# A chunked RWKV-7 recurrence feeding a cosine-gated unit, on one core: sign products in four column pieces, two loads in another order, three slots moved from one chunk to the next

## The chip, the cores and the metric

The kernel runs on one core of one Trainium2 chip. Its time is the device time of one execution in microseconds (us). Seven executions of the kernel before gave a median of 821.45 us (818.95 to 823.89). One further execution was taken with the hardware profiler; all views of the profile come from that one.

## The reference, cut to what matters

Two blocks in a row. The first is a recurrence over 768 time steps for 4 batches and 8 heads with a 40 x 40 state each; the second takes its output as 3072 tokens of 320 values.

```python
for t in range(S):                                    # r, k, v, w, a, b: (4, 8, 768, 40), float32
    y[:, :, t] = np.einsum('bhd,bhde->bhe', rt, state)
    Sa = np.einsum('bhde,bhe->bhd', state, at)
    state_decay = state * wt[:, :, None, :] - np.einsum('bhd,bhe->bhde', Sa, bt)
    state = state_decay + np.einsum('bhd,bhe->bhde', vt, kt)
...
x = np.ascontiguousarray(attn_out.transpose(0, 2, 1, 3)).reshape(B * S, H * D)
h = x @ w_in                                          # w_in: (320, 2048), float64
g = h * np.cos(h)
return (g @ w_out).astype(np.float32)                 # w_out: (2048, 320), float64
```

## The kernel before, in words

**Chunks.** The 768 steps are cut into 24 chunks of 32. Within a chunk the recurrence is written as small matrix products (heads and batches packed into the PE array) and one triangular inverse. `main(c)` (line 821) lists the five steps of a chunk: `ch_t` transposes the state `qz`, `ch_q` multiplies it with r, `ch_x` makes the right-hand side `x0`, `ch_s` (line 601) multiplies it with the inverse `rt`, `ch_z` (line 627) makes the new state and the output. In `ch_z`, DVE adds the PSUM result to `qz` (line 654), then POOL multiplies it by the chunk's decay (line 655), and the next chunk's `ch_t` needs that product.

**Preparation.** `p1(c)` (line 784) prepares two chunks at once from w, a and b: `p1_w` (line 358) transposes w (for chunks under 4 it also scans it on DVE), `p1_a` transposes a and takes the reciprocal of w (line 389) with the product b times reciprocal on POOL (line 390), `p1_b` transposes that product, `p1_n` multiplies both. `p2(c)` does the like for v, r and k. From chunk 4 on, w comes as a running product that `ws_scan` makes for four chunks at a time and stores to DRAM.

**The inverse.** `inverse(c)` (line 480) inverts the triangular matrices of four chunks together on DVE: one transpose, 31 steps of two DVE instructions (lines 466 and 470), one transpose back into `rt`. That of chunks 4 to 7 can start when `p1_n(6)` is done, and `ch_s(4)` needs its end.

**The second block** works on the 256 tokens of two chunks (a group g) and on a quarter j of the 2048 columns. It is cut into pieces, which run in one fixed order: `first_a(g, j)` and `first_b(g, j)` (8 and 16 matrix instructions into `ph`, then the cosine on ACT and DVE), and, once the next pair is under way, `second(g, j, 0)` and `second(g, j, 1)` (8 into `po` each). Below they are A(g,j), B(g,j), S(g,j)0 and S(g,j)1. A group may start only two chunks after its first chunk (`allowed`, line 914).

**The weights** come as float64. `rounded` (line 220) turns them into float32 in 20 work units of 128 x 512 values: a load of both 32-bit words, mantissa and exponent on DVE (lines 241, 242, 251) and ACT (lines 245, 254), the sign on ACT (line 247, a bf16 tile), the product of mantissa and exponent on DVE (line 257), and the product with the sign, in place, on POOL (line 260).

**The order of the work** is written by hand, and every engine runs its own instructions in that order. For each chunk a list `segs` (lines 924 to 960) names the steps; `M` is a slot for one piece of the second block. `step` (line 342) runs a step, then whatever was put off with `later(n, ...)`, then as many steps of the inverse and of the weights as `fill` says: (2, 3) in chunk 3, (2, 0) in chunk 4. Before `ch_s`, while `rt` is not there yet, the loop at line 972 takes further pieces, with four steps of the inverse each. Chunks above 3 have a goal for the pieces done by their end; by the end of chunk 5 it is 30.

**Loads.** `load(c, n)` (line 146) issues four DMAs of 40 KB, one per batch, by default on SP's queue. At the kernel's start SP issues w(0), w(1), then the six loads of line 186, then k, v and r of chunk 0; ACT issues a(0), a(1) and one load of w as a whole (`ws_fetch(1)`); POOL issues a(2) and a(3). A load into a buffer waits until its last reader is done: w(6) and w(7) follow the reciprocals of w(4) and w(5), and SP issues w(7), a(6), b(6), a(7), b(7) in this order.

Of the kernel before, what the change touches and what calls it, by code (L numbers as in the profile page):

```python
# [12 lines left out]
ALU = mybir.AluOpType  # L13
# [7 lines left out]
def kernel(  # L21
# [43 lines left out]
    nc = tc.nc  # L65
    B, H, S, D = r.shape
    P, C, DP = 128, 32, 64
# [52 lines left out]
    for n, fill in (("w", 1.0), ("a", 0.0), ("b", 0.0)):  # L120
        for i in range(4):
            x = slice((i - 2) * H * DP, (i - 1) * H * DP)
            if i < 2:
                t = const.tile([P, H, DP], F32, tag=f"nat_{n}{i}", name=f"nat_{n}{i}")
            else:
                t = {
                    "w": w_in_sb[:, 0, late:], "a": w_in_sb[:, 1, late:], "b": late_out
                }[n][:, x].rearrange("p (h d) -> p h d", h=H)
# [4 lines left out]
    for n in "kvr":  # L133
        t = const.tile([P, H, D], F32, tag=f"nat_{n}", name=f"nat_{n}")
# [11 lines left out]
    def load(c, names, via=nc.sync):  # L146
        for n in names:
            for i in range(B):
                at_c = src[n][i, :, c * C : (c + 1) * C, :]
                if n == "w" and c >= 4:  # L150
                    at_c = wd[c // 4][i, :, c % 4]
                via.dma_start(nat[n, c][blk[i], :, :D], at_c.rearrange("h t d -> t h d"))  # L152
# [6 lines left out]
    def ws_fetch(q, via=nc.sync):  # L159
        n = 4 * C * D  # L160
        via.dma_start(
            ws.rearrange("p t d -> p (t d)"),
            bass.AP(w.tensor, w.offset + q * n, [[S * D, B * H], [C * D, 4], [1, C * D]]),
        )

    def ws_scan(q):
        n = 1
        while n < C:
            to = ws[:, 2 * n - 1 :: 2 * n]
            nc.vector.tensor_tensor(to, to, ws[:, n - 1 :: 2 * n], ALU.mult)  # L170
            n *= 2
        n = C // 4
        while n:
            to = ws[:, 3 * n - 1 :: 2 * n]
            nc.vector.tensor_tensor(to, to, ws[:, 2 * n - 1 : C - 1 : 2 * n], ALU.mult)
            n //= 2
# [6 lines left out]
        load(c, "w")  # L183
        load(c, "a", nc.scalar)
    ws_fetch(1, nc.scalar)
    for n, c in (("b", 0), ("b", 1), ("w", 2), ("w", 3), ("b", 2), ("b", 3)):
        load(c, n)
    load(0, "kvr")

# [27 lines left out]
    WID = 512  # L217
    first_done, second_done = [], []

    def rounded(m, dst, src, by, by_sb):  # L220

        pool, tag = (
            ((sb2, "gT"), (sb2, "gT"), (sb1, "nt"), (sb1, "u"), (sb1, "inv"))[m % 5]
            if m < 10 else ((sb1, "nt"), (sb1, "u"), (sb1, "inv"))[(m - 10) % 3]
        )
        t = {}

        def fetch():  # L230
            t["words"] = pool.tile([P, WID, 2], I32, tag=tag, name="words")
            for rows, cols, part in src:
                nc.sync.dma_start(
                    t["words"][rows, cols].rearrange("p n w -> p (n w)"), part.bitcast(I32)
                )

        def taken():
            hi = t["words"][:, :, 1]
            t["mant"] = sb2.tile([P, WID], I32, tag="mant", name="mant")
            t["expo"] = sb2.tile([P, WID], I32, tag="expo", name="expo")  # L240
            nc.vector.tensor_scalar(t["mant"], hi, 0xFFFFF, None, ALU.bitwise_and)
            nc.vector.tensor_scalar(
                t["expo"], hi, 20, 0x7FF, ALU.logical_shift_right, ALU.bitwise_and
            )
            nc.scalar.activation(t["expo"], t["expo"], ACTF.Relu, bias=to_bits, scale=2.0**23)
            t["sign"] = sb2.tile([P, WID], mybir.dt.bfloat16, tag="sign", name="sign")
            nc.scalar.activation(t["sign"], hi, ACTF.Sign)

        def mantissa():
            frac = t["mant"].bitcast(F32)  # L250
            nc.vector.scalar_tensor_tensor(
                frac, t["words"][:, :, 0].bitcast(U32), 2.0**-32, t["mant"], ALU.mult, ALU.add
            )
            nc.scalar.activation(frac, frac, ACTF.Identity, bias=by_sb, scale=2.0**-20 * by)

        def product():
            nc.vector.tensor_tensor(
                dst, t["mant"].bitcast(F32), t["expo"].bitcast(F32), ALU.mult
            )
            nc.gpsimd.tensor_tensor(dst, dst, t["sign"], ALU.mult)  # L260

        return fetch, taken, mantissa, product

# [75 lines left out]
    def later(steps, work):  # L339
        waiting.append([steps, work])  # L340
# [465 lines left out]
    def scanned(q):  # L806

        ws_scan(q)
        later(2, lambda: ws_store(q))
        if q + 1 < NCH // 4:  # L810
            later(12, lambda: ws_fetch(q + 1))
# [17 lines left out]
    with tc.manual_schedule():  # L829
# [53 lines left out]
        v, k, g = p2(0)  # L883
# [33 lines left out]
        M = object()  # L917
        for c in range(NCH):
            t, q, x, s, z = main(c)
            v, k, g = p2(c + 1) if c + 1 < NCH else [lambda: None] * 3  # L920
            q0 = c - c % 4 + 4
            fill, pn, pn4 = (1, 4), None, None
            if c == 0:
                segs = [s, z]
            elif c == 1:
                segs = [t, v, q, k, x, g, s, z]
            elif c == 2:
                segs, fill = [t, v, q, k, M, x, M, g, M, s, M, z, M, M], (0, 2)
            elif c == 3:
                pw4, pa4, pb4, pn4 = p1(4)  # L930
                pw, pa, pb, pn = p1(6)
                segs = [
                    t, pw4, M, q, pa4, M, x, lambda: scanned(2), M, s, pw, M, pb4, pa, M, pn4, M, z, M,
                    pb, v, pn, k, M, g,
                ]
                fill = (2, 3)
            elif c == 4:
                pw, pa, *p8 = p1(8)
                segs = [t, v, M, q, M, k, x, M, g, M, M, M, s, pw, z, M, pa, lambda: scanned(3), M]
                fill = (2, 0)  # L940
            elif c == 5:
                pw, pa = p1(10)[:2]
                pb, pn = p8
                segs = [t, M, pb, q, M, pn, k, M, x, M, s, pw, v, M, z, M, g, M, pa, M]
            elif c % 4 == 0 and q0 < NCH:
                pb, pn = p1(q0)[2:]
                segs = [t, v, M, q, M, k, x, M, g, M, s, pb, M, z, M, pn, M, M]
                if q0 + 4 < NCH:
                    segs.insert(-1, lambda: scanned(c // 4 + 2))
            elif c % 4 == 1 and q0 < NCH:  # L950
                pw, pa = p1(q0 + 2)[:2]
                segs = [t, M, pw, q, M, x, k, M, s, v, M, z, M, pa, M, g, M, M]
            elif c % 4 == 2 and q0 < NCH:
                pb, pn = p1(q0 + 2)[2:]
                segs = [t, M, pb, q, M, pn, v, M, x, M, s, k, M, g, M, z, M, M]
            elif c % 4 == 3 and q0 + 4 < NCH:
                pw, pa = p1(q0 + 4)[:2]
                segs = [t, M, pw, q, M, x, k, M, s, v, M, z, M, pa, M, g, M, M]
            else:
                segs = [t, v, M, q, M, x, k, M, g, M, s, M, M, z, M, M]  # L960
            n = len(segs)

            goal = 8 * (c + 1) - (18 if c < 19 else 20)
            empty, places = 0, segs.count(M)
            if c > 3:
                empty = max(0, min(places - (goal - done), 2 if c < 8 else places))
                goal = max(goal, done + places - empty)
            place = 0
            if c == 19:
                shifted(N_PAD[c])  # L970
            for i, seg in enumerate(segs):
                while seg is s and ("rt", c) not in G:
                    if allowed(c):
                        piece(4, 0)
                    else:
                        inv_steps.pop(0)()
                while seg is pn4 and w_steps:
                    w_steps.pop(0)()
                if seg is not M:
                    step(seg, *fill, small=seg in (q, x, g, s, z, pn, pn4))  # L980
                    if c < 2 or c == 2 and not done:
                        busy({s: 6, q: 5, v: 4, k: 4, z: 4}.get(seg, 3))
                else:
                    place += 1
                    if place * empty // places > (place - 1) * empty // places:
                        continue
                    if allowed(c) and (c != 4 or done < 23):
                        piece(*fill)
                while i == n - 1 and c > 3 and done < goal and c != 4 and allowed(c):
                    piece(*fill)  # L990
                if seg is pn and (c == 3 or c > 4 and c % 4 == 2):
                    inv_steps.extend(inverse(q0))
# [36 lines left out]
```

## Time and profile before

| | |
|---|---|
| median of seven executions | 821.45 us |
| the profiled execution, its own time | 820.94 us |
| its span, first to last instruction | 819.2 us |
| mean granted TensorE clock | 0.953 |
| PE busy | 741.1 us, 90% |
| DVE busy | 509.6 us, 62% |
| ACT busy | 383.9 us, 47% |
| POOL busy | 201.0 us, 25% |
| the 20 sign products on POOL | 1.15 to 1.61 us each |

Of the PE's idle time, 68.5 us lie in the first 260 us and 9.6 us in the remaining 559. A row of a timeline has the start and the duration in us, the engine, the line, the operation, what it writes and reads, shapes and count; in brackets stand the idle time of the engine before it and what released it. Durations include the time in which an instruction is held up at its operands. "SPq" rows are the issuing of DMAs.

### The profile page before, as it was taken

What the parts mean: (1) busy time and instruction counts of PE and PEld (TensorE: products, weight loads), DVE (VectorE), ACT (ScalarE), POOL (GpSimd) and SP (SyncE); (2) the same over time, 40 slices, a digit from 0 to 9 for tenths busy, and PEclk for the clock granted to TensorE, in tenths of its full rate; (3) what the DMA queues carried; (4) which work ended last, traced back from release to release, by engine and by line L of the source; (5) the groups of instructions that cost most, each with busy time, mean ns of one, the idle gap of its engine ahead of it and who ended that gap; (6) DMA issues with size and microseconds to landing.
All of it is one profiled execution on the core that took longest, in us unless ns stands there. A gap on an engine that the chain in (4) does not pass through costs nothing.

```text
span 819.2 us, 37665 instructions
## 1 busy us (share of the span) xinstructions
PE 741.1 (90%) x16832; PEld 567.3 (69%) x16832; DVE 509.6 (62%) x1081; ACT 383.9 (47%) x707; POOL 201.0 (25%) x352
## 2 busy tenths in 40 slices
PE   3647778799688999999999999999999999999997
PEld 2533456677566777787777877877787777777775
DVE  6988888869644698454797553895445873332231
ACT  1214776554254545446345545435635435363352
POOL 5215554430203123221230330330230222201000
PEclk9757799999699999999999999999999999999999
DMA  7466553254043323334223324223220212101000
GB/s 120 69 147 175 162 150 118 47 126 69 25 101 87 68 45 63 63 95 77 50 39 69 67 62 69 60 43 68 53 42 23 45 37 53 22 17 37 20 17 16
DMA packets 183297, 55.66 MB, mean 68 GB/s; under 512 B 157152, under 2 KB 178656, under 8 KB 183136
## 3 DMA queue, kind: packets, MB, share of 16 engines
q1 hardware_dynamic: 180560, 51.95, 29.2%
q8 instruction: 132, 2.16, 1.1%
q10 hardware_dynamic: 2320, 0.98, 0.6%
q0 software_dynamic: 256, 0.33, 0.2%
q14 instruction: 29, 0.24, 0.1%
HBM read 42.07 MB, written 11.14 MB: 65 GB/s over the span
## 4 chain that ended last, share of the span: by engine, by line
PE 60%; DVE 20%; DMA 6%; ACT 5%; issue 3%; SPq 3%; POOL 2%; DVEq 0%; ACTq 0%; POOLq 0%
PE ph L101 21%; PE po L101 19%; DVE inv_tmp L466 4%; DVE inv L470 4%; PE dps L101 3%; PE x0ps L101 3%; SPq L152 3%; DVE rw L389 3%; PE gram L101 2%; PE vT L326 2%; PE sps L101 2%; DVE turns L730 1%; PE qps L101 1%; DMA xT<-xd 1%; PE nps L101 1%
## 5 line engine op out<-in xcount | busy, mean ns | idle before, releaser
L101 PE MATMUL po<-w_out_sb,gT 128*128 128x320 f32 x768 | 224.2, 440 | 0.0
L101 PE MATMUL ph<-xT,w_in_sb 128*128 128x256 f32 x768 | 186.5, 388 | 4.5 <-DVE gT L738 3.8
L101 PEld LDWEIGHTS po<-w_out_sb,gT 128*128 128x128 f32 x768 | 140.8, 191 | 55.0 <-issue 2.8
L101 PEld LDWEIGHTS ph<-xT,w_in_sb 128*128 128x128 f32 x768 | 140.8, 192 | 32.9 <-issue 13.8
L728 ACT ACTIVATE turns<-ph,rnd 128x512 f32<-128x512 f32 x96 | 63.9, 686 | 152.8 <-PE ph L101 152.4
L730 DVE SCALAR_TENSOR_TENSOR turns<-turns,ph 128x512 f32<-128x512 f32 x96 | 63.8, 684 | 107.5 <-ACT turns L728 107.1
L738 DVE TENSOR_TENSOR gT<-ph,turns 128x512 f32<-128x512 f32 x96 | 65.7, 686 | 36.1 <-ACT turns L735 36.1
L655 POOL TENSOR_TENSOR qz<-qz,wc 128x160 f32<-128x160 f32 x92 | 43.0, 485 | 161.0 <-DVE qz L654 160.2
L470 DVE TENSOR_TENSOR inv<-inv,inv_tmp 128x31 f32<-128x31 f32 (+15 forms) x186 | 72.6, 390 | 6.4
L466 DVE TENSOR_TENSOR inv_tmp<-u,inv 128x31 f32<-128x31 f32 (+15 forms) x186 | 70.4, 378 | 4.4
L734 ACT ACTIVATE turns<-turns 128x512 f32<-128x512 f32 x96 | 60.1, 626 | 24.6 <-DVE turns L730 24.6
L735 ACT ACTIVATE turns<-turns,half_pi 128x512 f32<-128x512 f32 x96 | 69.3, 722 | 3.1
L488 POOL COPY vp<-nat_v 128x320 f32<-128x320 f32 x25 | 12.1, 483 | 199.1 <-DMA nat_v<-in_v_dram 182.6
L101 PE MATMUL ph<-xT,w_in_tail 64*128 64x256 f32 x384 | 54.4, 402 | 0.0
L654 DVE TENSOR_TENSOR qz<-dps,qz 128x160 f32<-128x160 f32 x92 | 29.1, 317 | 32.1 <-PE dps L101 32.0
L560 ACT COPY s<-sT 128x512 f32<-128x512 f32 x46 | 24.5, 583 | 43.4 <-PE sT L556 43.4
L389 DVE RECIPROCAL rw<-nat_w 128x320 f32<-128x320 f32 x20 | 42.9, 2143 | 0.1
L101 PEld LDWEIGHTS ph<-xT,w_in_tail 64*128 64x128 f32 x384 | 33.0, 186 | 10.1 <-issue 6.5
L666 POOL TENSOR_TENSOR yt<-yt,wb 128x512 f32<-128x512 f32 x24 | 31.9, 1327 | 22.5 <-DVE yt L661 22.5
L544 ACT COPY vvm<-gram 128x256 f32<-128x256 f32 x24 | 8.8, 368 | 53.6 <-DVE ag L539 53.2
L101 PEld LDWEIGHTS sps<-x,rt 32*32 32x32 f32 x1536 | 18.5, 111 | 22.0 <-issue 15.8
L101 PE MATMUL sps<-x,rt 32*32 32x72 f32 x1536 | 23.6, 243 | 11.0 <-DVE rt L474 9.1
(118 smaller groups left out, 1068.4 us busy)
## 6 DMA issues: line engine op xcount, KB each, us to landing
words<-in_moe_w_in_dram SPq DMA_DIRECT2D x8, 512.0 KB
nat_k<-in_k_dram SPq DMA_DIRECT2D x96, 40.0 KB
nat_v<-in_v_dram SPq DMA_DIRECT2D x96, 40.0 KB
nat_r<-in_r_dram SPq DMA_DIRECT2D x96, 40.0 KB
xd<-yt SPq DMA_DIRECT2D x48, 80.0 KB
out_dram<-ot SPq DMA_DIRECT2D x24, 160.0 KB
nat_b<-in_b_dram SPq DMA_DIRECT2D x88, 40.0 KB
wd<-ws SPq DMA_DIRECT2D x5, 640.0 KB
```

What stands on the lines that cost most here:

```text
L101: nc.tensor.matmul(o, lhsT=lhsT, rhs=rhs, start=start, stop=stop, skip_group_check=True)
L389: nc.vector.reciprocal(rw, wn)
L466: nc.vector.tensor_tensor(tmp, u[:, j : j + 1, :j].to_broadcast([P, C - j, j]), x[:, j:, j : j + 1].to_broadcast([P, C - j, j]), ALU.mult,)
L470: nc.vector.tensor_tensor(x[:, j:, :j], x[:, j:, :j], tmp, ALU.subtract)
L654: nc.vector.tensor_tensor(z, pick(dp, 0, (2 * N72 + C, 2), (N72, 2), (1, D)), z, ALU.add)
L655: nc.gpsimd.tensor_tensor(z, z, wc.rearrange("p (f m b) -> p f m b", f=2, m=2)[:, :, :, bb] .unsqueeze(3).to_broadcast([P, 2, 2, D]), ALU. ...
L666: nc.gpsimd.tensor_tensor(yt.rearrange("p j b t -> p (j b) t"), yt.rearrange("p j b t -> p (j b) t"), wx, ALU.mult)
L728: nc.scalar.activation(n, u, ACTF.Identity, bias=rnd, scale=1.0)
L730: nc.vector.scalar_tensor_tensor(n, n, -ROUND, u, ALU.add, ALU.subtract)
L734: nc.scalar.activation(n, n, ACTF.Abs)
L735: nc.scalar.activation(n, n, ACTF.Sin, bias=half_pi, scale=-2.0 * math.pi)
L738: nc.vector.tensor_tensor(gT[:, 2 * e : 2 * e + 2].rearrange("p f t -> p (f t)"), us[e], ns[e], ALU.mult)
```

## The change

- **Sign products.** The one POOL instruction of 128 x 512 per weight unit becomes four of 128 x 128.
- **Loads at the start.** The order w(2), w(3) behind b(0), b(1) becomes w(2), b(0), w(3), b(1); b(2) and b(3) stay last.
- **Slots.** Chunk 3's list loses three of its eight slots (behind `pa4`, behind `pw`, behind `z`; the one behind `pn4` stands behind `v` afterwards). Chunk 4's list has five slots behind `g` and ahead of `s` instead of three.

```diff
-    for n, c in (("b", 0), ("b", 1), ("w", 2), ("w", 3), ("b", 2), ("b", 3)):
+    for n, c in (("w", 2), ("b", 0), ("w", 3), ("b", 1), ("b", 2), ("b", 3)):
         load(c, n)
...
-            nc.gpsimd.tensor_tensor(dst, dst, t["sign"], ALU.mult)
+
+            for o in range(0, WID, P):
+                x = dst[..., o : o + P]
+                nc.gpsimd.tensor_tensor(x, x, t["sign"][:, o : o + P], ALU.mult)
...
                 segs = [
-                    t, pw4, M, q, pa4, M, x, lambda: scanned(2), M, s, pw, M, pb4, pa, M, pn4, M, z, M,
-                    pb, v, pn, k, M, g,
+                    t, pw4, M, q, pa4, x, lambda: scanned(2), M, s, pw, pb4, pa, M, pn4, z, pb, v, M,
+                    pn, k, M, g,
                 ]
                 fill = (2, 3)
             elif c == 4:
                 pw, pa, *p8 = p1(8)
-                segs = [t, v, M, q, M, k, x, M, g, M, M, M, s, pw, z, M, pa, lambda: scanned(3), M]
+                segs = [t, v, M, q, M, k, x, M, g, M, M, M, M, M, s, pw, z, M, pa, lambda: scanned(3), M]
                 fill = (2, 0)
```

## The prediction

> **What bounds the kernel now.** I read the page's slices first, then busy time by stretch, then the timelines of the stretches in which the PE stands. The slices say where a change can count:
>
> ```profile
> PE   3647778799688999999999999999999999999997
> DVE  6988888869644698454797553895445873332231
> PEclk9757799999699999999999999999999999999999
> ```
>
> From slice 13 on the PE is full; only the first 260 us have slack. There DVE is the fuller engine until about 160 us, and the PE's largest stall comes at 204 us:
>
> ```profile
> 201.38 2.42 PE L101 MATMUL po<-w_out_sb,gT 128*128 128x320 f32 x8
> 211.35 1.25 PE L101 MATMUL sps<-x,rt 32*32 32x72 f32 x64 [7.56 <-DVE rt L474]
> 217.99 3.38 PE L101 MATMUL po<-w_out_sb,gT 128*128 128x320 f32 x8
> ```
>
> `ch_s(4)` waits 7.56 us for the inverse. The same 8 po instructions take 2.42 us ahead of the stall and 3.38 us behind it: the clock fell. Upstream, chunk 3 is paced by a load:
>
> ```profile
> 163.13 0.63 PE L326 MATMUL aps<-ident,nat_a 128*128 128x128 f32 x4 [1.83 <-DMA nat_a<-in_a_dram]
> ...
> 178.10 1.25 DVE L458 STREAM_TRANSPOSE u<-nt 128x1024 f32<-128x1024 f32 x1 [3.83 <-ACT nt L445]
> ```
>
> The second row is the start of the inverse; it ends at 211.20, and DVE is nearly gapless between. At the start, two loads set the pace:
>
> ```profile
> 13.44 3.90 SPq L152 DMA_DIRECT2D w_in_sb<-in_w_dram  x8
> 17.38 3.90 SPq L152 DMA_DIRECT2D w_out_sb<-in_b_dram  x8
> ...
> 19.20 1.11 PE L326 MATMUL wT<-ident,w_in_sb 128*128 128x128 f32 x4 [1.16 <-DMA w_in_sb<-in_w_dram]
> 20.86 2.34 DVE L370 TENSOR_TENSOR_SCAN wb<-wT,w 128x512 f32<-128x512 f32 x2
> ```
>
> From 20.86 DVE runs without a gap to the end of the first inverse at 64.2. Last, the sign products, with DVE around one of them:
>
> ```profile
> 80.47 0.68 DVE L251 SCALAR_TENSOR_TENSOR mant<-words,mant 128x512 f32<-128x512 uint32 x1
> 81.07 1.38 DVE L241 TENSOR_SCALAR mant<-words 128x512 int32<-128x512 int32 x1
> 82.37 0.41 DVE L242 TENSOR_SCALAR expo<-words 128x512 int32<-128x512 int32 x1
> ...
> 80.62 1.54 POOL L260 TENSOR_TENSOR w_in_tail<-w_in_tail,sign 128x512 f32<-128x512 f32 x1 [0.63 <-DVE w_in_tail L257]
> ```
>
> L241 takes 0.42 elsewhere and 1.38 here: it ends 0.29 after POOL does. Each has held up the other.
>
> **What the Trainium skill says.** "SBUF — State Buffer", section "Who interferes with whom": GpSimd and a DVE instruction in a two-port mode or with two SBUF inputs share a port pair, and the second to start is blocked for the whole instruction of the first. The rows above agree (0.96 us lost by L241). "GPSIMD Engine Reference", section 3.1: about 2.6 cycles per element at 1.2 GHz for a two-input product, an estimate of 1.11 us for 512; undisturbed L260 rows have 1.15 to 1.17. "TensorE: Matmul & The Clock Gate", section "What's actually happening": after one idle window of about 3.4 us the clock is halved until a busy window has passed. The trace agrees: granted 1.00 up to 206, 0.50 from 208 to 218, 1.00 from 220.
>
> **The change, part by part.**
>
> *Loads.* The last DMA of w(3) was the 16th after w(1) and becomes the 12th, at 15.4 instead of 17.3. It landed about 1.9 us after its issue, so wT comes at 17.3. DVE must finish aT of chunk 1 first (18.67), so the scan moves from 20.86 to about 18.9: 2.0 us. b(0) now ends where b(1) did, and its product started at 15.61 behind the reciprocal: no cost. b(1) lands at about 19.2 and its POOL product (18.21) goes 1.0 us later; `p1_b(0)` needs it at 25.4: nothing. b(2), b(3), k, v, r keep their places. The inverse ends 2.0 earlier, but the new state waits on POOL behind `rp` at 70.84, held by nat_r of chunk 2. That SP chain starts at 31.98, released by POOL's kn(0); kn(0) stands behind rp(0), whose r is issued until 27.2, so it moves 1.4 us only. I take **-1.4**; ends -2.0 and 0.
>
> *Sign products.* A line through L655 (160 columns, 0.44 us) and L260 (512, 1.16) gives 0.11 + 2.05 ns per column, or 0.37 for 128: 1.5 us per unit against 1.16, an estimate; if the fixed part vanished it would be 1.16, at L655's mean of 0.485 it is 1.94. POOL is 25% busy, so this counts only where the state queues behind it: once in each of chunks 0, 1, 2, +0.3 each. In chunk 1 ACT's order hides it (the copy of the state stands behind the mantissa at 106.22), so +0.6. For DVE, the four short qz products at 72.6 to 75.1 show what short POOL instructions do: L241, L242 and L257 took 0.26 longer and L251 0.09, alternating with them. POOL's quarter is 0.08 shorter, so I take four delays of 0.16 = 0.64 against 0.96. Eight units have this block (76.8, 80.6, 83.5, 86.8, 105.5, 109.4, 112.2, 139.7): 8 x 0.32 = 2.6, half of it on the path since ACT and DVE wait for each other in turn: -1.3. Together **-0.7**. Ends: every block gone and on the path, -7.7; four delays of the full 0.26 and 0.5 more POOL time per chunk, about +1.5.
>
> *Slots.* I wrote both orders out from the loop. Ahead of `p1_n(6)` chunk 3 ran A(0,2) to S(0,2)0; now it runs A(0,2), B(0,2), S(0,1)0, S(0,1)1. A(0,3), B(0,3), S(0,2)0 drop out there: 1.9 + 3.0 + 2.4 = 7.3 us of PE. But a(7) does not come earlier: SP issues w(7) once the reciprocal of w(5) ends (152.4), then a(6), b(6), a(7), and both S(0,1) pieces that covered this wait now follow it. So from 163.13 to nps(6), which took 12.56 us, there are left 12.56 - 0.29 idle - 7.3 + 4.8 = 9.8: -2.7. The PE idles some 4.6 us ahead of 163; if the clock falls, 1.35 comes back, I take half: -2.0. The inverse itself keeps its 33.1 us, plus one gT product (0.65) that B(1,1) gave later before: `ch_s(4)` comes 1.4 earlier. Pieces done by then: 21 before, 19 now, so B(1,1) and S(1,0)0, 5.5 us of PE, are owed. What takes this up: in chunk 5 two stalls of 1.34 and 1.06 (at 233.10 and 235.45) came from ACT standing behind B(1,2)'s cosine; now S(1,0)1 is in that slot, which gives ACT nothing: -2.4. The stall of 0.77 on xT at 259.04 gets two S pieces ahead of it: -0.8. The PE idle ahead of `ch_s(4)` shrinks from 7.56 by the one A more that lies there, 1.9, and grows by the 0.65 of the gT product: about 6.3. Behind it the clock was down to 220.5; with the shorter stall I choose that it comes back one window earlier, half of 3.4: -1.7. Sum: 5.5 - 1.4 - 2.4 - 0.8 - 1.7 = **-0.8**. Ends: no clock effect and no earlier `ch_s`, +3; the stall under a window so that the clock holds, -4. From chunk 6 on both orders are the same, and the PE there has 9.6 us of slack in all, so what is won or lost by then stays.
>
> Sum: -1.4 - 0.7 - 0.8 = -2.9, so 820.94 - 2.9 = **818.0 us**. The profiled execution lies 0.5 under the median of 821.45, inside its spread.
>
> **Rivals.**
> - *The gains are hidden:* the first 2 us vanish behind SP and POOL at 70.8, and the clock stays down as before. Then 0 - 0.5 + 0.9 (the slots' sum without 1.7): 821.3. For it: rp waits for nat_r, with the state behind it. Against: the SP chain hangs on kn(0), which does move.
> - *Slower, through chunk 3's load:* the PE loses its cover for a(7), idles over 3.4 us and starts chunk 3's second half at half clock. `ch_s(4)` then comes no earlier (0.65 later), and 5.5 us are owed: 5.5 + 0.7 - 2.4 = +3.8; with the loads hidden and half of the split's gain, -0.4: **824.3**. It decides as soon as the PE's idle time ahead of nps(6) grows by over 4 us. For it: 163.13 waits for this DMA already. Against: the remaining work there is 2.7 us shorter.
> - *The split does nothing:* if POOL keeps the port through four queued quarters, L241 waits 1.5 instead of 1.16, +0.3 x 8 for DVE, half of it on the path, +0.6 on POOL: +1.8 in place of -0.7, so 820.5, on the side of the first rival.
>
> **How the numbers follow.** Forecast 0.47, hidden or undone gains 0.29, slower 0.24. Under 0.3% (2.5 us) a measurement of this kernel can't tell from no change; the three cases lie on the three sides of it, so the chances are the same three. The range of 80% takes in both rivals, the split's good end in part and the clock's: 813.5 to 825.
>
> **What would show it.** Right: the first wT of w(3) at 17.3 and scan near 18.9; `rp` near 69.4; L241 under 0.8 beside sign products; u near 174 and sps(4) near 208, with a stall under 7 us; no stall at nps(8). Wrong: more than 5 us of PE idle ahead of aps(7), a sign quarter of 0.5 or more, or a clock of 0.5 through chunk 3.

## The result and the profile after

The kernel after the change takes 827.75 us (median of 12 executions, 824.51 to 829.81), against 821.45 (31 executions, 818.33 to 826.17). The ratio of after to before is 1.0067, 95% interval [1.0048, 1.0086]: 5.5 us slower, [3.9, 7.1], where 2.9 us faster was forecast. (This ratio, on record with its interval, is not exactly the quotient of the two medians, which differ by 6.3 us.) The measured median lies outside the forecast's range of 813.5 to 825. The profiled execution of the kernel after is the longest of the twelve, 829.81 us with a span of 828.1 and a mean granted clock of 0.947. Line numbers above 260 are three higher than before.

The page's slices first:

```profile
PE   3556688688699999999999999999999999999997
DVE  7986777838755499454698454895444774332231
PEclk9756999789899999999999999999999999999999
```

Counted from 0, the slices show the PE full from slice 11 on (before from 13), and yet the end comes later: what is lost lies ahead of that. The clock is down in slices 7 and 8 (145 to 186 us), where before it was at nine tenths or more; the drop in slice 10 is smaller than before.

In the timeline at the start, the transposes of w(2) and w(3) come without a wait, and the scan starts 2.05 us earlier than before, as forecast:

```profile
15.69 1.60 PE L329 MATMUL wT<-ident,w_in_sb 128*128 128x128 f32 x8
...
18.81 2.34 DVE L373 TENSOR_TENSOR_SCAN wb<-wT,w 128x512 f32<-128x512 f32 x2
```

Next comes the timeline of POOL where the first new state is made. `rp` (the copy of r for chunk 2) was forecast at 69.4, and four quarters of a sign product at 1.5:

```profile
71.81 0.58 POOL L491 COPY rp<-nat_r 128x320 f32<-128x320 f32 x1 [2.07 <-DMA nat_r<-in_r_dram]
72.36 2.83 POOL L263 TENSOR_TENSOR w_in_sb<-w_in_sb,sign 128x128 f32<-128x128 f32 x4
75.15 1.89 POOL L658 TENSOR_TENSOR qz<-qz,wc 128x160 f32<-128x160 f32 x4
```

The 2.0 us won on DVE are gone at `rp`, which waits for a load, and the quarters take 2.83. A little later, DVE and POOL side by side:

```profile
78.23 1.57 POOL L263 TENSOR_TENSOR w_in_sb<-w_in_sb,sign 128x128 f32<-128x128 f32 x4
...
81.90 2.85 POOL L263 TENSOR_TENSOR w_in_tail<-w_in_tail,sign 128x128 f32<-128x128 f32 x4
82.14 0.65 DVE L242 TENSOR_SCALAR expo<-words 128x512 int32<-128x512 int32 x1
82.71 0.91 DVE L257 TENSOR_TENSOR w_out_sb<-mant,expo 128x512 f32<-128x512 f32 x1
83.55 0.91 DVE L251 SCALAR_TENSOR_TENSOR mant<-words,mant 128x512 f32<-128x512 uint32 x1
84.39 0.65 DVE L241 TENSOR_SCALAR mant<-words 128x512 int32<-128x512 int32 x1
```

Alone, four quarters take 1.57, about as estimated. Beside DVE they take 2.85 where the one instruction took 1.54, and L241 takes 0.65 where it took 1.38. The quarters let DVE in between, and POOL pays. DVE itself gains next to nothing: the four DVE rows shown take 3.12 us together, and the same four beside one whole product took 3.15 before (1.38, 0.41, 0.68 and 0.68).

In chunk 3 before, B(0,2) ran ahead of x0, the right-hand side of `ch_x`, and S(0,1)1 ahead of the transposes bT of chunk 4. Neither x0 nor bT waited:

```profile
146.63 2.71 PE L101 MATMUL ph<-xT,w_in_sb 128*128 128x256 f32 x8
...
150.34 0.88 PE L101 MATMUL x0ps<-vvm,ag 32*32 32x72 f32 x64
...
156.92 2.32 PE L101 MATMUL po<-w_out_sb,gT 128*128 128x320 f32 x8
159.08 1.04 PE L326 MATMUL bT<-ident,bn 128*128 128x128 f32 x8
```

Chunk 3 and the wait for the inverse in the kernel after (x0, B(0,2), bT of chunks 4 and 6, S(0,1)1, the inverse's start, A(1,1), `ch_s(4)`):

```profile
152.31 1.26 PE L101 MATMUL x0ps<-vvm,ag 32*32 32x72 f32 x64 [2.68 <-ACT qz L575]
...
154.69 3.00 PE L101 MATMUL ph<-xT,w_in_sb 128*128 128x256 f32 x8
...
163.71 1.94 PE L329 MATMUL bT<-ident,bn 128*128 128x128 f32 x8 [3.12 <-ACT turns L737]
...
175.49 1.94 PE L329 MATMUL bT<-ident,bn 128*128 128x128 f32 x8 [1.09 <-DVE yt L664]
...
178.93 3.18 PE L101 MATMUL po<-w_out_sb,gT 128*128 128x320 f32 x8
...
184.60 1.25 DVE L461 STREAM_TRANSPOSE u<-nt 128x1024 f32<-128x1024 f32 x1 [8.40 <-ACT nt L448]
...
216.10 1.97 PE L101 MATMUL ph<-xT,w_in_sb 128*128 128x256 f32 x8 [3.10 <-DVE gT L741]
...
220.57 0.87 PE L101 MATMUL sps<-x,rt 32*32 32x72 f32 x64 [2.51 <-DVE rt L477]
```

Waits of 2.68 and 3.12 us stand where pieces ran before. The 8 instructions shown of B(0,2) take 3.00 and those of S(0,1)1 3.18, where at full clock such instructions take 1.9 to 2.4: the granted clock was 0.50 from 146.5 to 156.8 us and from 173.8 to 180.7. Before, S(0,1)1 took 2.32; B(0,2) took 2.71, because the clock was 0.50 there too, from 144.9 to 148.3. The inverse starts at 184.60, where 174 was forecast, and `ch_s(4)` comes at 220.57, where 208 was forecast. The PE waits for no load in this stretch.

Where the span's 8.9 us (828.1 - 819.2) come from, between the same PE instructions of both traces: +2.6 up to `ch_t(3)`, +3.8 from there to `p1_n(6)`, +2.9 to `ch_s(4)`, +1.5 to `ch_t(6)`, and -1.8 over all the rest. From two traces nobody can tell the first term from chance. Seven kernels with the same program up to there (the one before, e3, e5, e6, e7, e9, e14) had `ch_t(3)` between 136.88 and 141.25 us, and the kernel before happened to be the earliest. So stages are compared below from `ch_t(3)` on, and what lies ahead of it by medians alone.

For the stages I worked out a table: length, PE idle time in it, and clock loss, which is the PE's busy time in slices of about 1 us times one minus the granted clock. Length less idle and loss is the work at full clock. The experiments e3, e7, e14 and e9 are told below; each row is one trace.

| us: length / idle / clock loss | ch_t(3) to p1_n(6) | p1_n(6) to ch_s(4) | ch_s(4) to ch_t(6) |
|---|---|---|---|
| before | 38.8 / 6.7 / 1.7 | 35.7 / 8.0 / 0.0 | 45.9 / 4.6 / 3.9 |
| after | 42.6 / 12.1 / 7.6 | 38.5 / 8.5 / 0.0 | 47.4 / 1.9 / 3.0 |
| e3, slots alone | 43.7 / 12.7 / 8.1 | 38.0 / 6.6 / 1.5 | 44.3 / 1.3 / 0.0 |
| e7, B(0,2) first | 41.1 / 10.8 / 7.1 | 39.9 / 6.8 / 3.1 | 44.6 / 1.5 / 0.0 |
| e14, and a piece behind z | 39.0 / 9.5 / 6.0 | 36.9 / 6.8 / 0.0 | 47.1 / 1.7 / 3.0 |
| e9, slot behind pw alone | 45.4 / 9.7 / 7.5 | 38.3 / 6.3 / 1.6 | 42.1 / 3.7 / 0.0 |

In the first stage the work at full clock fell from 30.4 to 22.9 us, about the 7.3 us that the forecast took out. Idle time grew by 5.4 and clock loss by 5.9, and ate more than that.

How far single traces can be trusted here is shown by the eleven experiments whose chunk 3 is as before (e1, e2, e4, e8, e11, e12, e13, e15 to e18). Their first stage took 38.3 to 41.0 us, with 5.5 to 7.3 us idle and 1.5 to 4.1 of clock loss, and their second 35.6 to 36.3. The kernel after, e3 and e9 stand clear of that in both stages, e7 in the second; e14's first stage lies inside. The third stage took 44.1 to 48.1 in the eleven, so its length tells nothing.

### The profile page after: what moved, and what is told of

The parts are those of the page before. It is cut to its first block, busy times and chain, and to the rows that moved or that the text cites. A ratio compares the mean times of both kernels' runs of the same rounds, so it can differ in the third digit from the quotient of the medians.

```text
span 828.1 us, 37736 instructions
## 1 busy us (share of the span) xinstructions
PE 746.3 (90%) x16832; PEld 573.4 (69%) x16832; DVE 507.6 (61%) x1081; ACT 384.4 (46%) x707; POOL 215.6 (26%) x412
## 4 chain that ended last, share of the span: by engine, by line
PE 65%; DVE 19%; DMA 5%; ACT 4%; issue 3%; SPq 3%; POOL 2%; DVEq 0%; ACTq 0%; POOLq 0%
PE ph L101 23%; PE po L101 19%; DVE inv_tmp L469 4%; PE x0ps L101 4%; DVE inv L473 4%; PE dps L101 3%; PE gram L101 2%; PE vT L329 2%; SPq L152 2%; DVE rw L392 2%; PE sps L101 2%; PE nps L101 1%; PE qps L101 1%; DVE turns L733 1%; PE bT L329 1%
## 5 line engine op out<-in xcount | busy, mean ns | idle before, releaser
L101 PEld LDWEIGHTS ph<-xT,w_in_sb 128*128 128x128 f32 x768 | 141.1, 192 | 36.9 <-issue 17.9
L559 PE MATMUL sT<-ident,qz 128*128 128x128 f32 x184 | 26.4, 285 | 8.1 <-POOL qz L658 8.1
L101 PE MATMUL x0ps<-vvm,ag 32*32 32x72 f32 x1536 | 22.2, 235 | 11.6 <-ACT vvm L547 7.4
```

The costliest lines, as they stand in the source:

```text
L101: nc.tensor.matmul(o, lhsT=lhsT, rhs=rhs, start=start, stop=stop, skip_group_check=True)
```

## The experiments

All times are us against the kernel before on the same chip, from the ratio on record, with its 95% interval. As above, this ratio is not exactly that of the medians: for e1 it gives -1.4, while the medians differ by 0.75.

### The three parts

Each has one hunk of the change's diff: e1 the first (loads), e2 the second (sign products), e3 the third (both lists of slots); e4 has the first two. The line of each that says most:

```diff
+    for n, c in (("w", 2), ("b", 0), ("w", 3), ("b", 1), ("b", 2), ("b", 3)):
...
+                nc.gpsimd.tensor_tensor(x, x, t["sign"][:, o : o + P], ALU.mult)
...
+                    t, pw4, M, q, pa4, x, lambda: scanned(2), M, s, pw, pb4, pa, M, pn4, z, pb, v, M,
```

e1: 

> Only the loads' order is changed. Both theories: the scan of chunk 2 moves from 20.9 to 18.8 us and the first inverse ends 1.8 us earlier. Theory A (the slots cost the time, the loads bring their gain): 0.5 to 1.5 us under the kernel before. Theory B (the gain stops at POOL's rp of chunk 2, which waits for r): no change within 0.5 us.

e2: 

> Only the sign products are split. In the changed kernel four quarters took 1.57 us undisturbed and 2.8 us beside DVE, against 1.15 and 1.54. Theory A (slots): the split costs 1 to 2.5 us, as the state of chunks 0, 1 and 2 stands behind the quarters on POOL. Theory B (the split is the cause): 5 us or more.

e3: 

> Only the slots are moved. Theory A: most of the loss is here, 4 to 7 us over the kernel before, with the inverse of chunks 4 to 7 starting later although less PE work lies ahead of it. Theory B (split): within 1.5 us of the kernel before.

e4: 

> Loads and split, slots as before. Theory A: within 1.5 us of the kernel before. Theory B: 5 us over it. If the two parts meet (the earlier start lets the quarters fall beside more of DVE's work), it differs from the sum of the two single edits by over 1.5 us.

Measured: loads -1.4 [-2.6, -0.2]; split +2.6 [1.0, 4.3]; slots +4.9 [3.0, 6.7]; loads and split +1.4 [0.2, 2.6]. The three sum to +6.1 beside the +5.5 of the whole. So two parts lose, the slots probably more, and the loads do about what was forecast.

### Why the slots lose

Two theories. C: the slots of chunk 3 covered waits of its steps; uncovered, the PE stands and its clock halves. D: the slots only owe pieces behind `ch_s(4)`. e5, e9 and e6 each take one place out of chunk 3 and give it back in chunk 4 ahead of `ch_s(4)`, so that nothing is owed.

The lines of chunk 3 in e5, in e9 and in e6 (its next line is `pn, k, M, g`), and that of chunk 4 in all three:

```diff
-                    t, pw4, M, q, pa4, M, x, lambda: scanned(2), M, s, pw, M, pb4, pa, M, pn4, M, z, M,
+                    t, pw4, M, q, pa4, x, lambda: scanned(2), M, s, pw, M, pb4, pa, M, pn4, M, z, M,
+                    t, pw4, M, q, pa4, M, x, lambda: scanned(2), M, s, pw, pb4, pa, M, pn4, M, z, M,
+                    t, pw4, M, q, pa4, M, x, lambda: scanned(2), M, s, pw, M, pb4, pa, M, pn4, z, pb, v, M,
...
-                segs = [t, v, M, q, M, k, x, M, g, M, M, M, s, pw, z, M, pa, lambda: scanned(3), M]
+                segs = [t, v, M, q, M, k, x, M, g, M, M, M, M, s, pw, z, M, pa, lambda: scanned(3), M]
```

e5: 

> Only the slot behind pa4 leaves chunk 3; chunk 4 gets it back ahead of s, so as many pieces are done by ch_s(4) as before. Theory C (the slots of chunk 3 covered waits of its steps; without them the PE stands and its clock halves): x0 of chunk 3 waits some 3 us for ACT again, B(0,2) comes behind the scan and delays bT of chunk 4; +1.5 to +3 us over before. Theory D (the slots cost only because two pieces are owed behind ch_s(4)): nothing is owed here, so within 0.5 us of before.

e9: 

> Only the slot behind pw leaves chunk 3; chunk 4 gets one more ahead of s. S(0,1)1, which stood in front of bT of chunk 4, comes behind pa. Theory C (lost cover): the PE waits for a(7)'s load and bT with one piece less in front, +1 to +2.5 us over before. Theory D (only pieces owed behind ch_s(4) cost): within 0.5 us of before.

e6: 

> Only the slots behind pn4 and z of chunk 3 become one behind v; chunk 4 gets one more ahead of s. Theory C: z and bT of chunk 6 stand uncovered, PE idle some 2 us and half a window at half clock, +1 to +2.5 us. Theory D: within 0.5 us of before.

Measured: e5 +3.7 [1.8, 5.6], e9 +6.3 [4.0, 8.6], e6 +3.1 [1.6, 4.7]. In all three traces 21 pieces are done at `ch_s(4)`, as before, so D alone falls. But C's numbers were too small, and the three, with 13.1 in sum, don't add up to the 4.9 of the slots' part. Nor does e6's trace show where its loss lies: from `ch_t(3)` to `ch_t(6)` it took 120.3 us, against 120.4 before. The timeline of e9 shows the worst of them (bT of chunk 4, a(6), a(7), then S(0,1)1):

```profile
159.05 1.06 PE L326 MATMUL bT<-ident,bn 128*128 128x128 f32 x8 [1.21 <-ACT wb L374]
161.23 1.05 PE L326 MATMUL aps<-ident,nat_a 128*128 128x128 f32 x4 [1.11 <-DVE sm L620]
163.05 1.09 PE L326 MATMUL aps<-ident,nat_a 128*128 128x128 f32 x4 [0.77 <-DMA nat_a<-in_a_dram]
163.93 4.42 PE L101 MATMUL po<-w_out_sb,gT 128*128 128x320 f32 x8
```

There are three waits of about 1 us in a row, and the next piece runs at half clock: 4.42 where the same 8 instructions took 2.32 before. No wait is long; their closeness counts. The clock was halved at 161.34, behind the first two: in the 3.41 us ahead of that the PE was busy for 1.18 us. Before, the waits in this place (0.54 and 1.83) fell into two neighbouring stretches of 3.41 us, with 2.24 and 2.23 us busy, and the clock held. Such stretches are told of in the last section.

Next, the slots' part with two of its pieces put back over the waits of the fence of the kernel after. e7 leaves B(0,2) ahead of x; e14 also moves S(0,1)1 from behind v to behind z. Both take three places out of chunk 3 and owe two pieces at `ch_s(4)` (19 done, 21 before), as the slots' part does.

Against the slots' part, e7 and then e14:

```diff
-                    t, pw4, M, q, pa4, x, lambda: scanned(2), M, s, pw, pb4, pa, M, pn4, z, pb, v, M,
+                    t, pw4, M, q, pa4, M, x, lambda: scanned(2), s, pw, pb4, pa, M, pn4, z, pb, v, M,
+                    t, pw4, M, q, pa4, M, x, lambda: scanned(2), s, pw, pb4, pa, M, pn4, z, M, pb, v,
```

e7: 

> The slots' part, but with B(0,2) left ahead of x and of the scan; as many pieces are owed as in the slots' part. Theory C: the 3 us in front of x0 and the 2.3 us in front of bT of chunk 4 are covered again, the clock stays at 1.00 from 148 to 157; 2 to 3.5 of the slots' 4.9 us come back, so +1.5 to +3 over before. Theory D: unchanged at +4.9.

e14: 

> The slots' part with B(0,2) left ahead of x and of the scan, as in e7, and with S(0,1)1 behind z in place of behind v. Theory C: bT of chunk 6 does not wait for DVE's reads of z uncovered, the clock holds from 170 to 182, and 1 to 2 us more come back than in e7: +0.5 to +1.5 over before. Theory D (two pieces owed behind ch_s(4)): +2.6 as e7, or more.

Measured: e7 +2.6 [1.1, 4.0], e14 +0.3 [-1.2, 1.9]. With two pieces back over the waits, most of the slots' 4.9 us [3.0, 6.7] is gone, though as many pieces leave chunk 3 and as many are owed. So it is mainly the place of the pieces that costs, and not their number. The profiled execution of e14 is its longest, 829.49; from `ch_t(3)` to `ch_t(6)` the traces say +5.6 for e3, +5.2 for e7 and +2.7 for e14. The timeline of e3, the slots' part:

```profile
151.20 1.26 PE L101 MATMUL x0ps<-vvm,ag 32*32 32x72 f32 x64 [3.15 <-ACT qz L572]
...
153.59 3.78 PE L101 MATMUL ph<-xT,w_in_sb 128*128 128x256 f32 x8
...
175.38 1.94 PE L326 MATMUL bT<-ident,bn 128*128 128x128 f32 x8 [1.13 <-DVE yt L661]
...
178.82 3.52 PE L101 MATMUL po<-w_out_sb,gT 128*128 128x320 f32 x8
```

and of e14 (B(0,2), x0, then S(0,1)1 and bT of chunk 6):

```profile
150.47 3.30 PE L101 MATMUL ph<-xT,w_in_sb 128*128 128x256 f32 x8
...
154.76 0.88 PE L101 MATMUL x0ps<-vvm,ag 32*32 32x72 f32 x64
...
174.52 3.74 PE L101 MATMUL po<-w_out_sb,gT 128*128 128x320 f32 x8
178.09 1.04 PE L326 MATMUL bT<-ident,bn 128*128 128x128 f32 x8
```

x0 and bT of chunk 6 wait for nothing any more. The clock is still down under both pieces (clock loss 6.0 against 8.1), against the expectation: what helps is that the slow piece runs inside the wait and not behind it. In e14 x0 starts 13.5 us behind `ch_t(3)` with B(0,2) done; in e3 it starts after 12.7, and B(0,2)'s 4.8 us are still to come. In part the wait moves on: `ch_s(3)` now waits 2.65 us for ACT (0.32 before), because S(0,1)0 no longer stands there. Even so it comes 17.9 us behind `ch_t(3)`, as before (17.8), and not 19.8 as in e3.

Two further tries. e10 fills the waits of the slots' part with work that computes nothing, in unread columns of q's PSUM tile, to hold the clock; e11 takes the loads' part and moves S(1,0)1 into the PE's wait for the inverse, with chunk 3 as before.

In e10, behind the turns of a(4), a helper, and behind q's products of chunk 3; in e11 (the last two lines), beside the first hunk of the change:

```diff
+            if c == 4:
+                held(22)
...
+    def held(n):
+        for _ in range(n):
+            mm(G["spare"], idle, pick(idle, 0, (0, 2), (1, P)), False)
...
+        if c == 3:
+            G["spare"] = ps[:, 0, 2 * B * C :]
+            held(16)
...
-                segs = [t, v, M, q, M, k, x, M, g, M, M, M, s, pw, z, M, pa, lambda: scanned(3), M]
+                segs = [t, v, M, q, M, k, x, M, g, M, M, M, M, s, pw, z, M, pa, lambda: scanned(3), M]
```

e10: 

> The slots' part, with 38 idle bf16 products of 256 columns in chunk 3 (16 behind q, 22 behind the turns of a(4)), written to columns that nobody reads, where the PE waits for ACT. They do no work of the kernel. If the halved clock behind the waits is a cost of its own, B(0,2) takes 1.9 + 1.1 us again in place of 3.8 + 1.1 and 1.5 to 2.5 of the slots' 4.9 us come back: +2.4 to +3.4 over before. If only the waits themselves cost, +4.9 as before, or more.

e11: 

> The loads' part, with chunk 3 as before and one slot more in chunk 4 ahead of s: S(1,0)1 moves into the PE's wait for the inverse from behind z. If a slot in that wait is free, the 7.56 us of waiting shrink by 2.4 and as much is won: 2 to 2.5 us beside the loads' 1.4, -3.4 to -3.9 against before. If what is won there is lost at z of chunk 4, which the piece covered, -1.4.

Measured: e10 +15.4 [11.5, 19.3], e11 +1.5 [0.0, 3.0], which is worse than either of its expectations. e10 doesn't answer its question. Its second filler waited for ACT itself and then ran at half clock, in front of x0:

```profile
150.95 4.85 PE L101 MATMUL qps<-idle 128*128 128x256 bf16 x22 [3.55 <-ACT qz L581]
```

B(0,2) did get its clock back (1.99 + 1.13), but x0 came 4.8 us later behind `ch_t(3)` than in e3. e11 tells more. The wait at `ch_s(4)` shrinks from 7.53 (e1) to 5.89, and from there to `ch_t(5)` 1.7 us are won. Then, in chunk 5 (nps, kT, S(1,1)1):

```profile
233.73 1.36 PE L101 MATMUL nps<-aT,bT 40*32 40x32 f32 x128 [2.17 <-ACT bT L427]
236.08 1.12 PE L326 MATMUL kT<-ident,kn 128*128 128x128 f32 x4 [0.99 <-ACT qz L572]
236.99 4.48 PE L101 MATMUL po<-w_out_sb,gT 128*128 128x320 f32 x8
```

The PE reaches the same ACT-bound place earlier, waits 2.17 instead of 1.34 there, and this tips the clock: S(1,1)1 takes 4.48 instead of 2.32. In the 3.41 us ahead of the drop at 234.66 the PE was busy for 1.25 us; in e1 the two stretches at this place had 2.07 and 2.35, and the clock held. From `ch_s(4)` to `ch_t(6)` the clock loss is 6.8 against 3.4 in e1. In these two traces a gain on the PE became idle time, and the idle time cost more than the gain.

### Why the split loses

Two theories. E: POOL's quarters hold the sign tile longer; it has two buffers, so ACT's sign of two units later waits for POOL, and the copies behind it on ACT are late. F: POOL's longer time in front of the state's product costs by itself. ACT's signs in e2, and x0 of chunk 1 behind them, in e2 and then in the kernel before:

```profile
80.92 0.70 ACT L247 ACTIVATE sign<-words 128x512 bf16<-128x512 int32 x1 [0.39 <-POOL w_in_sb L263]
85.63 0.67 ACT L247 ACTIVATE sign<-words 128x512 bf16<-128x512 int32 x1 [1.78 <-DMA xT<-xd]
91.72 0.68 ACT L247 ACTIVATE sign<-words 128x512 bf16<-128x512 int32 x1 [0.34 <-POOL w_out_sb L263]
```

```profile
87.41 1.26 PE L101 MATMUL x0ps<-vvm,ag 32*32 32x72 f32 x64 [3.25 <-ACT qz L575]
```

```profile
85.28 0.88 PE L101 MATMUL x0ps<-vvm,ag 32*32 32x72 f32 x64 [1.73 <-ACT qz L572]
```

No sign waits in the trace of the kernel before; in e2 ACT stands 3.2 us in front of four of them. (The 1.78 are put down to a DMA that the sign doesn't read; the quarters of two units before end at 85.59, just ahead of it.) x0 waits 3.25 for the copy behind the second of these signs, and before it waited 1.73. Two ways to take the wait away: three buffers (e8, e18), or the sign issued one step later (e13, e15); each with its control whose sign products are whole (e12, e17; e16).

e8 and e13 have the split alone, e12 neither hunk, e15 and e18 loads and split, e16 and e17 the loads. The third buffer (first two pairs of lines; the output tile makes room for it) and the later sign (from `taken` to the end of `mantissa`):

```diff
-            t["sign"] = sb2.tile([P, WID], mybir.dt.bfloat16, tag="sign", name="sign")
+            t["sign"] = sb3.tile([P, WID], mybir.dt.bfloat16, tag="sign", name="sign")
...
-            ot = sb2.tile([P, DM], F32, tag="ot", name="ot")
+            ot = sb2.tile([P, WID], F32, tag="expo", name="ot")[:, :DM]
...
-            nc.scalar.activation(t["sign"], hi, ACTF.Sign)
...
+            nc.scalar.activation(t["sign"], t["words"][:, :, 1], ACTF.Sign)
```

e8: 

> The split sign products, with three buffers for the sign tile in place of two (the output tile shares the exponents' buffers to make room). Theory E (POOL's quarters beside DVE hold the sign tile for 2.8 us in place of 1.5, ACT's next sign waits for it, and the copies queued behind it on ACT are late): no wait of ACT on POOL, x0 of chunk 1 waits under 2.3 us, 1.5 to 2.5 of the split's 2.6 us come back: 0 to +1 over before. Rival F (the longer POOL time itself, ahead of the state's product): the sign buffers change nothing, +2.6.

e12: 

> The kernel before with three buffers for the sign tile, sign products unsplit (the control of e8_split_sign3). Theory E: in the kernel before no sign waits for POOL, so within 0.5 us of before. If the third buffer is a gain by itself, -1 us or more, and the split costs more than e8 showed.

e13: 

> The split sign products, with ACT's sign of a unit issued one step later (beside the mantissa's scaling, after the product of the unit before), so that its tile's last reader on POOL is two units back. Two buffers as before. Theory E (ACT waits for POOL through the sign tile): no wait of a sign for POOL, and 1.5 to 2.5 of the split's 2.6 us come back: 0 to +1.2 over before. Rival F (POOL's longer time ahead of the state's product): +2.6 as the split alone.

e15: 

> Loads and split, with the sign one step later as in e13. The loads' -1.4 plus what e13 gives. Theory E: -1.4 to 0. Rival F: +1.4 as e4. If DVE's relief by the quarters is worth something once ACT's wait is gone, below e16.

e16: 

> Loads with the sign one step later, sign products whole: the control of e15, and the candidate for the fastest kernel. The later sign takes no wait away here, so -1.4 as the loads alone, within 1 us.

e17: 

> Loads with three buffers for the sign tile, sign products whole: the control of e18, and a candidate for the fastest kernel. -1.4 as the loads alone, within 1 us.

e18: 

> Loads and split with three sign buffers. Theory E (the split costs only through the sign tile): within 1 us of e17, at best 0.7 below. Rival F (POOL's longer time costs by itself): 2 to 2.8 us above e17, as e4 stood above the loads alone.

| | whole | split | split - whole |
|---|---|---|---|
| two buffers | 0 | e2 +2.6 [1.0, 4.3] | +2.6 |
| two buffers, loads | e1 -1.4 [-2.6, -0.2] | e4 +1.4 [0.2, 2.6] | +2.8 |
| three buffers | e12 -0.2 [-2.0, 1.6] | e8 +0.8 [-1.2, 2.8] | +1.0 |
| three buffers, loads | e17 0.0 [-1.4, 1.4] | e18 +0.7 [-0.8, 2.1] | +0.7 |
| sign later, loads | e16 +1.5 [-0.3, 3.2] | e15 +0.6 [-0.9, 2.1] | -0.9 |
| sign later | not run | e13 +2.7 [1.4, 4.0] | |

No sign waits for POOL in e8, e13, e15 or e18, and x0 of chunk 1 waits 1.29 in e18:

```profile
84.48 0.88 PE L101 MATMUL x0ps<-vvm,ag 32*32 32x72 f32 x64 [1.29 <-ACT qz L575]
```

Where signs wait, the split costs 2.6 and 2.8; where they don't, 1.0, 0.7 and -0.9, a mean of +0.3. Each difference is uncertain by about 2 to 3 us, so this speaks for E and doesn't prove it. e13 by itself speaks for F; but its control e16 lost as much against e1 as the split did, so the later sign probably costs something of its own, and why stays open.

No version is clearly faster than the kernel before. The loads alone came nearest (-1.4, or 0.75 by the medians), and with three sign buffers (e17) they gave 0.0, where -1.4 was expected.

## Why the prediction was wrong

Between the -2.9 that was forecast and the +5.5 that was measured lie 8.4 us. By the single parts the slots make 5.7 of them (-0.8 forecast, +4.9 measured), the split 3.3 (-0.7 and +2.6) and the loads nothing; the parts' sum is 0.6 above the whole.

**Loads: right in size, by a path that isn't shown.** -1.4 was forecast and -1.4 measured. Four further pairs with and without it give -1.2 (e4 - e2), +0.2 (e17 - e12), -2.1 (e15 - e13) and -0.1 (e18 - e8), a mean of all five of -0.9. The scan and the inverse did come 2 us earlier (`ch_s(0)` at 62.09 in e1, 64.36 before). But the 1.4 us were to come out at `rp`, and there e1 is no earlier than before (70.84):

```profile
71.13 0.46 POOL L488 COPY rp<-nat_r 128x320 f32<-128x320 f32 x1 [1.86 <-DMA nat_r<-in_r_dram]
```

With `rp` varying by more than that from run to run (below), one trace can't show where the gain comes out. The rival "the gains are hidden" was right about `rp` in the kernel after (71.81), and had neither of the two losses. (The reading that DVE runs "without a gap" up to 64.2 was loose: its gaps add up to 3.5 us there, the longest 0.44.)

**Split: wrong in sign, through the term "POOL is 25% busy, so this counts only where the state queues behind it".** POOL's 1.5 us per unit came out at 2.07 on average (37.2 us for the 18 units of `w_in_sb` and `w_out_sb`; 1.41 before), at 2.83 beside DVE: I used the price of undisturbed quarters for POOL and the disturbed rows for DVE alone. DVE's relief was there on L241, by the groups of the traces before and after:

```profile
L241 DVE TENSOR_SCALAR mant<-words 128x512 int32<-128x512 int32 x20 | 17.3, 863 | 0.0
```

```profile
L241 DVE TENSOR_SCALAR mant<-words 128x512 int32<-128x512 int32 x20 | 11.2, 561 | 0.0
```

That is 6.1 us less on this line. Its neighbours take longer beside quarters (L251 0.91 for 0.68). In e2, the split alone, L241 gives 5.8 us and L242, L251 and L257 take 3.9 of them back. DVE's busy time in all fell from 509.6 to 507.6 us after, near the forecast's 2.6. It made nothing earlier that can be seen in the times. And I left out a reader: the sign tile is released by POOL, and an ACT sign two units later, with the state's copies in line behind it, waits for that. The waits are in the traces; that they make up the +2.6 isn't proven. The rival "the split does nothing" had this sign but another mechanism, since POOL does let DVE in.

**Slots: wrong, at the step "-2.7" and "-2.0" for `p1_n(6)`.** The 7.3 us of PE work did leave, and `p1_n(6)` came 4.9 later in e3. I subtracted PE work as if the PE set the pace there. The steps of chunk 3 wait for ACT, DVE and POOL in turn, and the pieces ran beside those waits; I priced each removed piece as time on the path, and the ones moved in as cover for a(7)'s load, without asking which waits the removed ones had covered. Of the clock I said "I take half"; in e3 the clock loss was 6.4 more than before in this stretch. "The inverse itself keeps its 33.1 us, plus one gT product" was off too: +2.3 us in e3 from `p1_n(6)` to `ch_s(4)`. In the kernel after, where it is +2.9, part of that is visible (DVE waits 1.45 for gram, ahead of which the PE stands 1.99 for nothing that the profile shows); the rest is open. The chunk-5 and xT terms were right: no stall at `p1_n(8)` or on xT, and less idle time behind `ch_s(4)` (1.3 against 4.6). The shorter stall ahead of `ch_s(4)` was right too: 5.6 us of PE idle time after (3.10 and 2.51), 6.3 forecast.

**The slower rival** had the deciding sign right (PE idle time ahead of `p1_n(6)` grew by over 4 us, and the clock was at half) and the mechanism wrong: a(7)'s load is waited for neither after nor in e3. Its 824.3 lacked the split's loss and most of the clock's. Two of the prediction's own signs of being wrong came true: a sign quarter took 0.52 to 0.58 us on average, and the clock was at 0.50 in three parts of chunk 3.

## What to carry to other kernels

A piece of filler work is not worth its own duration but the wait that it covers; before moving one, name the wait in each place, and on what engine the step behind it hangs. Waits of 1 us close together can halve the PE's clock and cost more than the idle time itself (in e9's first stage idle time is 3.0 us more than before and clock loss 5.8 more), so a gain that only lets the PE arrive earlier at the same wait may be a loss. When an instruction gets slower on an idle engine, look at who waits for the buffers that it releases, not only at who needs its result.

## What the runs showed of the hardware

- **POOL and DVE alternate instruction by instruction.** In the kernel after, the ends of a DVE instruction and of a POOL quarter take turns: 82.22 and 82.51 us, 82.79 and 83.08, 83.62 and 83.91, 84.46 and 84.75. Four quarters of 128 columns take 1.57 alone and 2.85 beside DVE; L241 takes 0.42 alone, 0.65 beside quarters and 1.38 beside a whole product. This fits the Trainium skill, "SBUF — State Buffer", section "Who interferes with whom" (the second is blocked for the whole instruction of the first): a quarter alone is 0.39, and L241 loses 0.23, less than one. The alternation costs POOL more than it saves DVE on that instruction: +1.31 against -0.73.
- **The clock follows the PE's busy share over fixed stretches of 3.41 us, and no stretch has to be idle.** In every trace the changes of the granted clock lie whole multiples of 3.41 us apart, on a grid that lies differently from run to run. Before, the clock was halved at 206.32, behind a stretch with 0.90 us of PE busy time, and came back at 219.97, behind a full one; it had stayed down behind one with 2.64. So "one idle window" in the prediction was too strict. Over the first 290 us of all twenty traces, the PE was busy, as the profile models it, for 0 to 72% of the stretch ahead of each of the 157 drops, for 41% or more of every stretch behind which the clock held, and for 81% or more ahead of each return. Between 41 and 72% both happened, and why is open. So where the grid falls decides whether two short waits share a stretch, and in this the clock loss of a single trace is partly luck.
- **The start differs from run to run of one program.** SP took 1.87 to 3.45 us to issue the four DMAs of v of chunk 2, and `rp`, which waits for r behind them, came at 70.84 before and at 74.61 in e14, whose program is the same up to there:

```profile
66.42 3.45 SPq L152 DMA_DIRECT2D nat_v<-in_v_dram  x4
69.91 1.95 SPq L152 DMA_DIRECT2D nat_r<-in_r_dram  x4
```

```profile
74.61 0.49 POOL L488 COPY rp<-nat_r 128x320 f32<-128x320 f32 x1 [2.16 <-DMA nat_r<-in_r_dram]
```

- **PE waits for nothing that the profile shows** came more often in e10, with 38 more PE instructions: behind 240 us eight of over 0.5 us, 9.4 us in sum, against one of 1.23 before. Much of its 15.4 us lies there; the cause is open.
